# Attention and MLP-mixer on one core: the opening of batches 0 to 2 put in another order (masks sooner, V2 of both heads in one slot, q and k regrouped ahead of the last channel-mix items, part of the kT copies on VectorE)

## The chip, the cores and the metric

The kernel runs on one core of one Trainium2 chip. The time of a run is the device time of that core in microseconds. Each kernel was run several times, always beside runs of the kernel before on the same chip. A run counts as slow when it is over 1.5% longer than the fastest of the same kernel. A difference of less than 2% gets the verdict "same"; a 95% interval goes with every ratio, so that smaller differences can be told apart too.

## The reference, cut to what matters

Eight batches, eight heads, 576 positions, head width 64. Attention with a sliding window of 128 and an ALiBi bias, then an MLP-mixer on its output:

```python
scores = scale * q @ k.T + bias            # rel in [0, 128) only, else -1e9
attn   = exp(scores - max) / sum
x      = attn @ v                          # put back to (batch, 576, 512)
u      = x + (relu(x.T @ w_tok1) @ w_tok2).T      # token mix
out    = u + relu(u @ w_ch1) @ w_ch2              # channel mix
```

## The kernel before: the parts that the change touches

A *group* is one pair of heads of one batch: groups 0 to 3 are batch 0, 4 to 7 batch 1, 8 to 11 batch 2. The kernel runs the attention of one batch beside the mixer of the batch before it. TensorE instructions of the two are interleaved by `spread`, which puts the items of a side list between those of a main list by their costs. In the traces each engine's instructions come in the order in which they are written.

Names in code and traces: `pe` are the exponentials of the scores and `pb` the same times the mask (a mask product), `xb` is the normalized attention output, `ub` is `u` (its sum with the token mix) and `UT` its transpose, which the channel mix reads. V2 stands for the V matmuls of group 2 with their normalization. A relu eviction takes a finished block of the channel mix out of PSUM.

For batches 0 to 2, q and k come in over the software DMA queue, are regrouped by VectorE (L152), transposed by TensorE (L214) and copied out of PSUM (L226, L227). From batch 3 on, the transposes are done by DMA, which also needs the regrouped data.

```python
def regroup(b, h0, h1, which=(0, 1)):              # VectorE, L152
    for n in which:
        raw, t = ((qn, qg), (kn, kg))[n]
        nc.vector.tensor_copy(out=t[:RP, :, h0:h1, :], in_=raw[b % 2]...)   # cut

def att_T(g, early=False):
    ...                                            # 6 + 6 transposes per group
    nc.scalar.copy(out=dst[0], in_=src[0])                              # qT, ScalarE
    (nc.scalar.copy if early or b == 2 else nc.vector.tensor_copy)(out=dst[1], in_=src[1])  # kT

def att_V(g, early=False):
    ...                                            # V matmuls, reciprocal, product
    if hp == NHP - 1 and b + 2 < B:                # last group of a batch:
        for c in range(NF):
            dma_v(b + 2, c)                        # its v loads, 2 batches ahead
        dma_v_tail(b + 2)
```

After the opening (batch 0's attention, written out by hand), the channel mix of batch 0 (`c1`) runs beside the attention of batch 1, then the mixer of batch 1 (`its1`) beside that of batch 2:

```python
n0 = 9
for _, f in c1[:n0]:
    f()                                            # channel matmuls alone
side = [(0.0, lambda: regroup(1, 0, H))]
if B > 3:
    side.append((0.0, lambda: dma_qk(3, 0, H)))    # loads of q and k of batch 3
side += [(0.6, lambda: att_T(g)), (0.6, lambda: att_T(g + 1))]
...                                                # scores, transposes, V of batch 1
spread(c1[n0:] + its1[: n1 - 3], side)
for _, f in its1[n1 - 3 : n1]:
    f()
regroup(2, 0, H)

g = 2 * NHP
side = [(0.6, lambda: att_T(g)), (0.6, lambda: att_T(g + 1))]
side += score_items(g)
side += [(0.6, lambda: att_T(g + 2)), (0.6, lambda: att_T(g + 3))]
for n in range(2):
    side.append((0.3, lambda n=n: regroup(3, 0, H, (n,))))
    side.append((0.0, lambda n=n: dma_trans(3, (n,))))
side.append((0.0, lambda: dma_qk_behind(4, 3)))    # q, k of batch 4 once tk(3) is in
...
spread(its1[n1:], side)
```

The softmax here doesn't subtract the row's maximum and nothing guards it: scores larger than these inputs give would overflow.

## Time and profile before

| | |
|---|---|
| median of 3 runs | 313.87 us (313.83 to 314.05) |
| TensorE busy | 93% of a span of 311.7 us |
| VectorE, ScalarE busy | 56%, 59% |
| TensorE idle from 16 to 80 us | 10.1 us |
| granted TensorE clock | 1.00 in every stretch |

The prediction below shows the totals, the table of stretches and the stalls at the transposes. In a table of stretches each line is: the stretch, its length, then busy time (and instructions) of TensorE, weight loads, VectorE, ScalarE and GpSimd, then granted clock, DMA share and GB/s. In a timeline each line is: start, duration, engine, line, operation, output and inputs, count, and in brackets how long the engine was idle just before and what released it.

Three further stalls of TensorE between 40 and 54 us turned out to matter later. They are behind ScalarE's exponentials (`pe`) and VectorE's normalization (`xb`):

```profile
41.84 0.40 PE L246 MATMUL sp<-qT,kT 64*128 64x256 bf16 x4 [0.29 <-ACT pe L258]
...
43.58 0.40 PE L246 MATMUL sp<-qT,kT 64*128 64x256 bf16 x6 [0.76 <-ACT pe L258]
...
53.54 0.73 PE L300 MATMUL ot<-vp,pb 128*128 128x65 bf16 x18 [0.71 <-DVE xb L318]
```

### The profile page before, as it was taken

How to read it: one execution, taken by the hardware profiler on the slowest of the kernel's cores; microseconds unless marked ns; L12 is line 12 of the kernel's file. 1: busy time of each engine (PE TensorE's matmuls, PEld its weight loads, DVE VectorE, ACT ScalarE, POOL GpSimd, SP SyncE). 2: the span in 40 equal slices, each digit the busy share in tenths (PEclk: the TensorE clock that was granted, in tenths of full speed). 3: DMA queues.
4: the chain of work that ended last, by engine and by line, in shares of the span. 5: the costliest groups of instructions: out<-in, count | busy, mean ns of one | idle time of the engine just before them, and what ended most of it. 6: DMA issues, size and time to landing. Idle time of an engine off the chain costs nothing.

```text
span 311.7 us, 6394 instructions
## 1 busy us (share of the span) xinstructions
PE 290.3 (93%) x2645; PEld 182.8 (59%) x2669; DVE 176.0 (56%) x341; ACT 185.1 (59%) x371; POOL 61.8 (20%) x85
## 2 busy tenths in 40 slices
PE   6877888898999999999999999999999999999995
PEld 2465655455764467645774467645774477547743
DVE  6695667658466865378733865378434753262021
ACT  3974496185997438854896438853996338304700
POOL 8993242600202500540013000500000000000000
PEclk9999999999999999999999999999999999999999
DMA  7999999998596997699649027781101110101022
GB/s 95 151 181 205 201 169 171 194 102 180 94 159 128 190 144 124 99 218 198 138 78 109 34 91 107 90 80 68 37 0 36 67 69 0 36 34 70 0 69 101
DMA packets 83005, 33.64 MB, mean 108 GB/s; under 512 B 62048, under 2 KB 78496, under 8 KB 82976
## 3 DMA queue, kind: packets, MB, share of 16 engines
q0 software_dynamic: 54224, 17.90, 56.2%
q1 hardware_dynamic: 28752, 15.34, 20.0%
q8 instruction: 21, 0.34, 0.5%
q14 instruction: 8, 0.07, 0.1%
HBM read 35.78 MB, written 9.44 MB: 145 GB/s over the span
## 4 chain that ended last, share of the span: by engine, by line
PE 66%; ACT 20%; DVE 9%; issue 4%
PE o L471 26%; PE ct L439 20%; ACT pe L258 10%; ACT R L450 5%; PE ot L300 4%; PE ht L376 4%; PE sp L246 3%; PE t L363 3%; ACT qT L226 2%; DVE pb L269 2%; PE ut L426 2%; ACT r1t L368 2%; DVE xb L311 1%; PE wt L597 1%; DVE qg L152 1%
## 5 line engine op out<-in xcount | busy, mean ns | idle before, releaser
L258 ACT ACTIVATE pe<-sp,biascol 128x512 bf16<-128x512 f32 x128 | 80.7, 705 | 47.0 <-PE sp L246 47.0
L439 PE MATMUL ct<-UT,WC 128*128 128x288 bf16 x768 | 103.0, 286 | 2.8 <-ACT R L450 2.1
L471 PE MATMUL o<-WC,R 128*128 128x512 bf16 x402 | 99.2, 379 | 1.0
L439 PEld LDWEIGHTS <-WC 128*128 128x128 bf16 x768 | 72.5, 98 | 25.0 <-issue 5.7
L450 ACT ACTIVATE R<-ct 128x288 bf16<-128x288 f32 x180 | 67.2, 434 | 32.4 <-PE ct L439 28.1
L269 DVE TENSOR_TENSOR pb<-pe,masks 128x1024 bf16<-128x1024 bf16 x64 | 44.0, 688 | 47.9 <-ACT pe L258 47.9
L471 PEld LDWEIGHTS <-R 128*128 128x128 bf16 x420 | 39.0, 98 | 42.0 <-issue 0.9
L137 POOL DMA_DIRECT2D vp<-in_v_dram x28 | 25.7, 935 | 74.0 <-PE ot L300 63.2
L380 DVE TENSOR_TENSOR ub<-ht,xb 128x512 bf16<-128x512 f32 x35 | 24.0, 688 | 14.9 <-PE ht L376 14.8
L483 DVE TENSOR_TENSOR obt<-o,ub 128x512 f32<-128x512 f32 x31 | 21.3, 687 | 17.2 <-PE o L471 17.2
L300 PEld LDWEIGHTS <-pb 128*128 128x128 bf16 x576 | 21.8, 98 | 6.5 <-DVE xb L318 0.8
L300 PE MATMUL ot<-vp,pb 128*128 128x65 bf16 x576 | 23.4, 194 | 1.2 <-DVE xb L318 0.7
L246 PE MATMUL sp<-qT,kT 64*128 64x256 bf16 (+2 forms) x320 | 21.5, 250 | 3.1 <-ACT pe L258 1.5
L226 ACT COPY qT<-tq 128x576 bf16<-128x576 bf16 x20 | 24.2, 1208 | 0.0
L318 DVE TENSOR_TENSOR xb<-ot,rt 128x640 bf16<-128x640 f32 x28 | 23.1, 825 | 1.0
L246 PEld LDWEIGHTS <-kT 64*128 64x128 bf16 x320 | 12.5, 94 | 17.0 <-issue 12.0
L376 PE MATMUL ht<-r1t,W 128*128 128x512 bf16 x66 | 20.5, 379 | 0.8 <-ACT r1t L368 0.7
L368 ACT ACTIVATE r1t<-t 128x512 bf16<-128x512 f32 x14 | 8.4, 600 | 16.0 <-PE t L363 15.9
L363 PE MATMUL t<-xb,W 128*128 128x512 bf16 x69 | 16.2, 379 | 0.1
L317 DVE RECIPROCAL rt<-ot 128x10 f32<-128x10 f32 x28 | 6.1, 217 | 15.6 <-PE ot L300 15.6
L431 DVE COPY UT<-ut 128x576 bf16<-128x576 bf16 x28 | 11.5, 450 | 4.8 <-PE ut L426 4.8
L479 DVE COPY obt<-o 128x512 f32<-128x512 f32 x4 | 2.8, 692 | 19.7 <-PE o L471 19.7
(68 smaller groups left out, 200.7 us busy)
## 6 DMA issues: line engine op xcount, KB each, us to landing
out_dram<-obt SPq DMA_DIRECT2D x31, 256.0 KB, 2.1
qn<-in_q_dram POOLq DMA_DIRECT2D x7, 576.0 KB, 11.8
kn<-in_k_dram POOLq DMA_DIRECT2D x7, 576.0 KB, 14.3
vp<-in_v_dram POOLq DMA_DIRECT2D x28, 128.0 KB, 11.3
WC<-in_moe_w_ch_dram POOLq DMA_DIRECT2D x3, 512.0 KB, 7.7
WC<-in_moe_w_ch_dram POOLq DMA_DIRECT2D x1, 1536.0 KB, 22.5
out_dram<-obt SPq DMA_DIRECT2D x10, 128.0 KB, 2.4
vp<-in_v_dram POOLq DMA_DIRECT2D x16, 64.0 KB, 5.4
```

Source lines behind the costliest of these rows:

```text
L137: nc.gpsimd.dma_start(out=vp[b % 2][:, :, c, 0:D], in_=v[b, :, c * P : (c + 1) * P, :].rearrange("h s d -> s h d"),)
L226: nc.scalar.copy(out=dst[0], in_=src[0])
L246: nc.tensor.matmul(sp[:, hh, i * 256 + x0 : i * 256 + x1], lhsT=kt[r, k0 : k0 + P], rhs=qt[r, q0 : q0 + x1 - x0], start=True, stop=True,)
L258: nc.scalar.activation(out=pe[:, i, :], in_=sp[:, i, :], func=ACT.Exp, bias=biascol[:, h : h + 1], scale=scale,)
L269: nc.vector.tensor_tensor(out=pb[:, :, :].rearrange("p h (k x) -> p h k x", k=2), in0=pes.pop((g, half))[:, :, :].rearrange("p h (k x) -> ...
L300: nc.tensor.matmul(ots[i][:, qb * (D + 1) : (qb + 1) * (D + 1)], lhsT=pb[:, i, col : col + P], rhs=vb[:, h, kc, :], start=(n == 0), stop=( ...
L363: nc.tensor.matmul(t1[:, :], lhsT=W1[:, c, dh * P : (dh + 1) * P], rhs=xb[b][:, c, :], start=(c == 0), stop=(c == NCH - 1),)
L376: nc.tensor.matmul(ht[:, :], lhsT=W2[:, j, c0(c) : c0(c) + P], rhs=r1s[b, j][:, :], start=(j == 0), stop=(j == NDH - 1),)
L380: nc.vector.tensor_tensor(out=ubs[b][:, c, :], in0=ht[:, :], in1=xb[b][:, c, :], op=ALU.add)
L439: nc.tensor.matmul(ct[:, :], lhsT=WC1[:, cb, ht_i * P : (ht_i + 1) * P], rhs=UT[:, cb, o : o + SH], start=(cb == 0), stop=(cb == NCB - 1),)
L450: nc.scalar.activation(out=r2, in_=ct[:, :], func=ACT.Relu)
L471: nc.tensor.matmul(o2[0][:, :], lhsT=R2[:, ht_i, col : col + P], rhs=WC2[:, ht_i, :], start=(ht_i == 0 and c != NF), stop=(ht_i == NHT - 1),)
```

## The change

Its intent is to take work off the path that TensorE waits for in the first 75 us: masks of the last two groups sooner on VectorE, kT copies from ScalarE to VectorE where ScalarE is the busier, regroupings before the work that they can hide behind. The core of the diff (the opening cut to the order of its calls):

```diff
-        (nc.scalar.copy if early or b == 2 else nc.vector.tensor_copy)(out=dst[1], in_=src[1])
+        on_act = g in (0, 3, 10, 11)
+        (nc.scalar.copy if on_act else nc.vector.tensor_copy)(out=dst[1], in_=src[1])
 ... the copy of UT out of PSUM: batch 0's last one goes to VectorE
-        (nc.vector.tensor_copy if b else nc.scalar.copy)(
+        (nc.scalar.copy if b == 0 and cb < NCB - 1 else nc.vector.tensor_copy)(
 ... opening
+        build_masks(2)
         att_M(0, 1)
         att_T(2, True)
-        build_masks(2)
 ...
+        build_masks(3)
         att_M(1, 1)
         att_T(3, True)
         att_V(0, True)
-        build_masks(3)
 ...
-        att_V(2, True)
         trans_u(0, 0)
+        att_M(3, 1)
+        att_V(2)
         tok2_pair(1)
-        att_M(3, 1)
 ... (tok1_pair(3), tok2_pair(3), trans_u(0, 2), trans_u(0, 3) reordered alike)
 ... batch 1
-        n0 = 9
+        n0 = 11
 ...
-        spread(c1[n0:] + its1[: n1 - 3], side)
-        for _, f in its1[n1 - 3 : n1]:
+        spread(c1[n0:] + its1[: n1 - 2], side)
+        regroup(2, 0, H)
+        for _, f in its1[n1 - 2 : n1]:
             f()
-        regroup(2, 0, H)
 ... batch 2
-        side = [(0.6, lambda: att_T(g)), (0.6, lambda: att_T(g + 1))]
-        side += score_items(g)
-        side += [(0.6, lambda: att_T(g + 2)), (0.6, lambda: att_T(g + 3))]
+        side = [(0.3, lambda n=n: att_T(g + n, n % 2 == 1)) for n in range(NHP)]
         for n in range(2):
-            side.append((0.3, lambda n=n: regroup(3, 0, H, (n,))))
+            side.append((0.2, lambda n=n: regroup(3, 0, H, (n,))))
             side.append((0.0, lambda n=n: dma_trans(3, (n,))))
         side.append((0.0, lambda: dma_qk_behind(4, 3)))
+        side += score_items(g)
```

More of the change, by code (lines that the diff above doesn't have):

```diff
@@ L647 @@
         att_M(3, 0)
-        att_V(2, True)
         trans_u(0, 0)
+        att_M(3, 1)
+        att_V(2)
         tok2_pair(1)
-        att_M(3, 1)
+        att_V(3, True)
         tok1_pair(2)
-        att_V(3, True)
         trans_u(0, 1)
+        tok1_pair(3)
         tok2_pair(2)
-        tok1_pair(3)
+        tok2_pair(3)
         trans_u(0, 2)
-        tok2_pair(3)
+        trans_u(0, 3)
         nc.vector.tensor_copy(out=swap[:, 0:TAIL], in_=ident[:, TAIL:P])
         nc.vector.tensor_copy(out=swap[:, TAIL:P], in_=ident[:, 0:TAIL])
-        trans_u(0, 3)
         c1, its1 = mixer_items(0)[-2 * NHT :], mixer_items(1, lead=2)
         n1, g = 6, NHP
-        n0 = 9
+        n0 = 11
         for _, f in c1[:n0]:
```

## The prediction

> **What bounds the kernel now.** I read the engine totals first, then the busy tenths by slice, then stretches of the span, then the order of single instructions where TensorE is idle, and last the DMA issues with their times to landing.
>
> From the page, the totals (busy us, share) and the slices (7.8 us each, tenths busy):
>
> ```profile
> PE 290.3 (93%) x2645; PEld 182.8 (59%) x2669; DVE 176.0 (56%) x341; ACT 185.1 (59%) x371; POOL 61.8 (20%) x85
> ...
> PE   6877888898999999999999999999999999999995
> ...
> DMA  7999999998596997699649027781101110101022
> ```
>
> TensorE is the bound after slice 9, and the DMA engines are nearly full up to slice 9. All the edits act before about 76 us, so they can only remove TensorE idle time there. The stretches (PE is the second number after the length) say how much there is:
>
> ```profile
> 16.00:24.00 8.00, 5.66 (x105) 4.92 (x105) 7.83 (x22) 5.93 (x12) 8.00 (x12) 1.00 1.49 184
> 24.00:32.00 8.00, 6.15 (x79) 4.88 (x80) 3.93 (x11) 3.17 (x7) 2.67 (x4) 1.00 1.29 204
> 32.00:40.00 8.00, 6.87 (x74) 4.83 (x72) 5.33 (x9) 4.19 (x9) 1.37 (x2) 1.00 1.24 203
> 40.00:48.00 8.00, 6.84 (x77) 4.74 (x76) 5.74 (x11) 7.60 (x16) 4.21 (x5) 1.00 2.20 167
> 48.00:56.00 8.00, 7.18 (x104) 4.48 (x105) 6.64 (x14) 3.77 (x8) 1.55 (x2) 1.00 2.30 159
> 56.00:64.00 8.00, 6.57 (x49) 3.19 (x49) 3.80 (x6) 2.95 (x6) 5.27 (x5) 1.00 1.64 210
> 64.00:72.00 8.00, 7.08 (x65) 3.97 (x66) 6.40 (x10) 5.20 (x9) 0.00 (x0) 1.00 1.01 89
> 72.00:80.00 8.00, 7.57 (x85) 4.97 (x84) 5.34 (x11) 5.47 (x12) 0.00 (x0) 1.00 0.88 181
> ```
>
> Eight minus the PE numbers: 2.34, 1.85, 1.13, 1.16, 0.82, 1.43, 0.92, 0.43; sum 10.1 us. That is the ceiling. Two per cent of 313.87 is 6.3 us, so a clear win needs well over half of it. From 16 to 24 VectorE is busy 7.83 of 8: it is what TensorE waits for. From 40 to 48 ScalarE is (7.60 of 8).
>
> The single stalls, from TensorE's timeline (bracket: idle before, and releaser):
>
> ```profile
> 30.03 4.69 PE L439 MATMUL ct<-UT,WC 128*128 128x288 bf16 x37 [0.36 <-ACT UT L431]
> 35.16 0.43 PE L214 MATMUL tT<-ident,qg 96*128 96x96 bf16 x6 [0.44 <-DVE qg L152]
> 36.28 0.43 PE L214 MATMUL tT<-ident,kg 96*128 96x96 bf16 x6 [0.70 <-DVE kg L152]
> ...
> 59.94 0.43 PE L214 MATMUL tT<-ident,qg 96*128 96x96 bf16 x6 [0.57 <-DVE qg L152]
> 61.18 0.43 PE L214 MATMUL tT<-ident,kg 96*128 96x96 bf16 x6 [0.81 <-DVE kg L152]
> ...
> 71.53 0.23 PE L422 MATMUL ut<-swap,ub 128*128 128x128 bf16 x1 [0.79 <-DVE ub L380]
> ```
>
> The regroupings of batch 1 (35 us) and batch 2 (60 us) each stall the transposes that read them. Last, the two loads of batch 3 that the change wants sooner, from the DMA issues between 48 and 52 us (last number: median us to landing):
>
> ```profile
> qn<-in_q_dram POOLq DMA_DIRECT2D x1, 576.0 KB, 13.1
> ...
> kn<-in_k_dram POOLq DMA_DIRECT2D x1, 576.0 KB, 15.5
> ```
>
> Issued at 48.43 and 50.44, they land at about 61.5 and 65.9. I return to this under step 4.
>
> **What the Trainium skill says.** "Perfetto Trace Analysis", Optimizing Scalar/DVE Operations: an access to PSUM costs VectorE some 125 ns and ScalarE some 51 ns. The trace agrees in sign: the copy of a transposed 128x576 tile out of PSUM takes 0.76 us on VectorE (kT) and 0.64 us on ScalarE (qT). So moving kT copies is no saving of work, only of ScalarE's place in line. "DMA: Bandwidth & Descriptors", Queues, rings and completion order: each DMA engine serves its queues in turn, packet by packet. So a hardware transpose beside the software queue slows both; before, the first transposes (70.86 us) come when the software queue is nearly empty (10 GB/s in 68 to 70), so the trace neither confirms nor denies it. "TensorE: Matmul & The Clock Gate", What's actually happening: about 3.4 us of idleness halves the clock. No stall in this trace is that long, and the clock reads 1.00 in every stretch.
>
> **The change part by part.** I followed the order of the changed kernel's instructions on each engine and put the durations of this trace on them by hand.
>
> *Step 1, first scores (0 to 17 us).* Two kT copies (groups 1 and 2) leave ScalarE: each took about 0.53 us start to start there. Exponentials wait for them, so the third group's first exponential starts some 0.6 us sooner (13.8 instead of 14.4). But VectorE gains two copies (0.67 start to start), and the masks of heads 6 and 7 (six instructions, about 0.68 us start to start when undisturbed, 11.83 to 12.51 for the pair before) now stand ahead of the first normalization. Summing VectorE's queue from 9.3 us: copy 9.95, mask product 10.56, regrouping 11.17, masks 11.85, product 12.45, copy 13.12, product 13.72, regrouping 14.28, masks 14.96, product 15.57, then four normalizing instructions (1.26): 16.85 against 16.57 before. Nothing gained for the first token-mix matmul, some 0.3 us lost.
>
> *Step 2, token mix of batch 0 (17 to 30 us).* Masks are out of the way, the two products of group 3 sit together, V2 in the shared slot needs one reciprocal and one product (0.98 us start to start) instead of two of each (1.26), and the third token-mix matmul no longer stands ahead of V3. Following the chain: second half of group 3's scores 19.3 (19.45 before), its products done 21.85, V2 normalized 22.9, ub of pair 1 23.65, V3 normalized 24.9 (25.9 before), pair 3's ub 27.7 (28.7 before), transposes of the last column block 28.3, UT copy on VectorE about 0.45 instead of 0.64. The channel mix then runs freely at 28.8 instead of 30.03: **1.2 us gained.**
>
> *Step 3, batch 1.* Before, 40 channel matmuls come ahead of the first transposes; now 48, and VectorE's order puts six relu evictions (four before) ahead of the regrouping. At 0.1225 us each 45 matmuls from 28.8 end near 34.4, so the regrouping starts at 34.85 (34.15 before), q is ready at 35.8 and k at 36.95. The stall is about 1.4 + 0.8 = 2.2 us against 1.14: **the 1.1 us comes back off.** Eight more matmuls are done, though, so first exponential is only 0.6 later (39.65 against 39.06). The stretch from there is ScalarE's: 16 exponentials at 0.575, two q copies at 0.55 and now four instead of six evictions at 0.3, so it ends near 51.2 instead of 51.77. Then the regrouping of batch 2 stands ahead of the last eight channel matmuls and the first tok1: VectorE's normalizations end at 56.4, q and k are ready at 57.4 and 58.5, and TensorE arrives at 57.95. Stalls of 0.57 + 0.81 shrink to some 0.1. By the first-group transposes of batch 2 TensorE is at 58.9 where it had been at 61.6: **2.5 us gained in all,** of which 1.2 from step 2 and about 1.3 from the moved regrouping.
>
> *Step 4, batch 2.* All four transposes now come before the scores, with two of the four kT copies on VectorE, and the regrouping of batch 3 directly behind. VectorE works in order, and its order is now: q of batch 3, first ub, **k of batch 3**, four ub with two products and one eviction between. k cannot start before its load lands at 65.9, whatever TensorE does, as the DMA queue ahead of it is full from the start. From there: regrouping 1.0 (66.9), two ub 1.2 (68.1), product, eviction, product 1.8 (69.9), two ub 1.2, so **the u transposes start near 71.3, against 71.53 before.** TensorE reaches them at about 68.2 and waits some 3 us. So most of the 2.5 us is spent on waiting for a load that nobody waited for before (k was regrouped at 71.39). What remains is work done ahead: group 9's scores before u, group 8's V and group 10's scores before the channel mix. From 71.3 the blocks add up to a channel mix at 75.35; twelve matmuls (1.47) bring it to 76.85, and the same content was reached at 78.42 before. **Net 1.6 us.**
>
> Behind 80 us nothing is removed. ScalarE was 9.94 of 10 busy from 80 to 90; with two groups of exponentials already done, part of TensorE's 0.3 + 0.38 us idle up to 100 may go: 0.2.
>
> **The rivals.**
> (a) The 2.5 us carries through, because k lands sooner or the ub work hides it: 311.3 or a little less. For it: a stall that I place by hand could be short. Against it: landing is set by a queue full from 4 us on.
> (b) The wait becomes worse. The transpose of q of batch 3 now starts near 63.2, beside the last 2.7 us of the load of k. If they share engines packet by packet, k lands 1 to 2 us later, everything after it too, and the gain is gone: 313.5 to 314.5. A stall of 5 us could moreover halve the clock for a window: about 1.7 us more, an estimate from the skill's 3.4 us. Against it: the load may be nearly over, and the transpose's first packets come late.
> (c) The kT copies make VectorE the bound in the first 25 us and step 2 gives nothing. VectorE is already 7.83 of 8 busy there. It matters little to the end if step 4's wait stands, which absorbs the loss as it absorbs the gain.
>
> **Range and chances.** Steps 1 to 4 give 1.6 + 0.2 = 1.8, so 312.1 if the load of k is undisturbed. I take off about 0.5 for (b), half likely at around 1 us: **312.6 us.** Rival (a) with an extra microsecond gives the lower end, 310.7; (b) in full the upper one, 314.4. Faster by over 2% means under 307.6, half of all idle time there gone: 0.04. Slower by over 2% means 320.1, which needs both parts of (b) several times over: 0.02.
>
> **What would show it.** Right: the free-running channel mix of batch 0 starts near 28.8; the stalls at the batch 1 transposes grow to about 2 us; those at batch 2's vanish; kg's third large copy starts at 66 to 67 with VectorE idle before it, released by the DMA; the u transposes of batch 1 start near 71.3 after about 3 us of idle TensorE. Wrong: u transposes at 69 (then (a)) or at 73 and later (then (b)); a start of the channel mix at 29.5 or later (then (c)).

## The result, and the profile after

| | median | range | runs | ratio to before, 95% |
|---|---|---|---|---|
| before | 313.94 us | 313.83 to 314.05 | 4 | |
| changed | 311.97 us | 310.94 to 312.50 | 4 | 0.9933 (0.9906 to 0.9960) |

All runs were fast ones, though one of the changed kernel had a clock of 0.994 (312.50). A ratio is the mean time of one kernel's fast runs over that of the other's in the same rounds, so it isn't quite the ratio of the medians. The change is worth 0.7%, some 2 us. That is a real gain, close to the predicted 312.6.

What follows first is the profiled run of the changed kernel (312.24 us), the one that the prediction's working can be laid beside. In the changed kernel's profile, line numbers from L227 on are one higher than before. TensorE is busy 290.9 us (94% of a span of 310.4). The stretches of the changed kernel, columns as before:

```profile
16.00:24.00 8.00, 6.58 (x124) 5.62 (x124) 7.41 (x17) 5.24 (x11) 8.00 (x13) 1.00 1.31 150
24.00:32.00 8.00, 6.46 (x72) 5.09 (x70) 3.94 (x10) 3.36 (x8) 2.72 (x4) 1.00 1.28 204
32.00:40.00 8.00, 5.89 (x63) 4.25 (x62) 5.35 (x9) 2.91 (x8) 1.92 (x2) 1.00 1.23 195
...
56.00:64.00 8.00, 7.66 (x80) 4.60 (x78) 6.23 (x9) 4.15 (x8) 4.92 (x5) 1.00 1.62 197
64.00:72.00 8.00, 5.76 (x41) 2.49 (x41) 6.14 (x11) 5.19 (x9) 0.00 (x0) 1.00 1.87 133
72.00:80.00 8.00, 7.95 (x102) 6.04 (x102) 5.86 (x13) 4.26 (x11) 1.73 (x3) 1.00 0.91 188
```

TensorE's busy time rose from 5.66 to 6.58 in 16 to 24, from 6.57 to 7.66 in 56 to 64 and from 7.57 to 7.95 in 72 to 80. It fell from 6.87 to 5.89 in 32 to 40, and from 7.08 to 5.76 in 64 to 72. So the time won in two places was partly spent in two others. TensorE's timeline says on what:

```profile
28.87 5.67 PE L440 MATMUL ct<-UT,WC 128*128 128x288 bf16 x45 [0.18 <-DVE UT L432]
...
35.96 0.43 PE L214 MATMUL tT<-ident,qg 96*128 96x96 bf16 x6 [1.41 <-DVE qg L152]
37.08 0.43 PE L214 MATMUL tT<-ident,kg 96*128 96x96 bf16 x6 [0.70 <-DVE kg L152]
...
59.57 0.43 PE L214 MATMUL tT<-ident,kg 96*128 96x96 bf16 x6 [0.29 <-DVE kg L152]
...
68.28 1.02 PE L472 MATMUL o<-WC,R 128*128 128x512 bf16 x4 [0.70 <-DVE ub L381]
...
71.88 0.23 PE L423 MATMUL ut<-swap,ub 128*128 128x128 bf16 x1 [1.49 <-DVE ub L381]
```

The free-running channel mix starts at 28.87 instead of 30.03. The stalls of the first transposes of batch 1 grow from 0.44 + 0.70 to 1.41 + 0.70. Those of batch 2 shrink from 0.57 + 0.81 to 0.29. Then come two waits for `ub`, 0.70 and 1.49, where there was one of 0.79. VectorE's timeline tells why `ub` is late. It sat idle before the regrouping of k of batch 3, and what ended that was a DMA:

```profile
63.26 0.95 DVE L152 COPY qg<-qn 96x3072 bf16<-96x3072 bf16 x1 [1.13 <-PE tT L214]
...
66.67 0.95 DVE L152 COPY kg<-kn 96x3072 bf16<-96x3072 bf16 x1 [1.86 <-DMA kn<-in_k_dram]
```

And the chain of waits, followed back from the end (start, length, what), now runs through two loads, q of batch 2 (issued at 32.26) and k of batch 3 (issued at 51.48, when q had landed), into the `ub` additions and the `u` transposes:

```profile
32.26 18.66 DMA qn<-in_q_dram
...
51.48 15.10 DMA kn<-in_k_dram
...
66.67 0.95 DVE kg L152
```

Over the whole span that chain is put down as 61% TensorE and 17% DMA. Before it was 66% TensorE, 20% ScalarE and 9% VectorE, with no DMA at all.

To compare many kernels I cut the span at three landmarks. A is the start of the free-running channel mix of batch 0, u the first `u` transposes of batch 1, D the first matmul of batch 1's shared last output chunk. From D to the end all kernels took 218.7 to 218.8 us (one took 219.6, told below), so everything happens ahead of D.

| profiled run | A | A to u | u to D | A to D | idle at batch 1's first transposes | clock of the run |
|---|---|---|---|---|---|---|
| before | 30.03 | 41.50 | 21.47 | 62.97 | 1.14 | 1.000 |
| changed | 28.87 | 43.01 | 19.74 | 62.75 | 2.11 | 1.000 |
| changed, again | 29.73 | 42.83 | 19.74 | 62.57 | 1.85 | 0.994 |

From A to D the changed kernel is only 0.2 us shorter in this run, so nearly all of the profiled run's 1.3 us had been won before A. Of the rest, 1.7 us come from u to D and 1.5 are lost again from A to u.

### The profile page after: what moved, and what is told of

Same layout as the page of the kernel before. It is cut to its first block, busy times and chain, and to the rows that moved or that the text cites. A ratio compares the mean times of both kernels' runs of the same rounds, so it can differ in the third digit from the quotient of the medians.

```text
span 310.4 us, 6391 instructions
## 1 busy us (share of the span) xinstructions
PE 290.9 (94%) x2645; PEld 183.3 (59%) x2669; DVE 179.1 (58%) x344; ACT 182.0 (59%) x366; POOL 61.5 (20%) x85
## 4 chain that ended last, share of the span: by engine, by line
PE 61%; DMA 17%; ACT 13%; POOL 4%; issue 2%; DVE 2%; POOLq 0%; DVEq 0%
PE o L472 25%; PE ct L440 18%; DMA qn<-in_q_dram 10%; DMA kn<-in_k_dram 7%; ACT pe L259 5%; ACT R L451 5%; PE ht L377 4%; PE ot L301 4%; PE t L364 3%; PE sp L247 3%; PE ut L427 2%; ACT qT L226 2%; ACT r1t L369 2%; POOL vp L143 1%; PE o2h L497 1%
## 5 line engine op out<-in xcount | busy, mean ns | idle before, releaser
L381 DVE TENSOR_TENSOR ub<-ht,xb 128x512 bf16<-128x512 f32 x35 | 23.9, 687 | 10.6 <-PE ht L377 10.5
L319 DVE TENSOR_TENSOR xb<-ot,rt 128x640 bf16<-128x640 f32 x29 | 23.9, 824 | 1.0
```

What stands on the lines that cost most here:

```text
L319: nc.vector.tensor_tensor(out=xs, in0=o4[:, :, :, 0:D], in1=rt[:, :, :, None].broadcast_to([P, 2, NCH, D]), op=ALU.mult,)
```

## The experiments

Twelve kernels ran, one of them the changed kernel again, in three calls (kernel before in each: medians 313.78, 313.69 and 313.45 us). The first two calls were on one chip and the third on another. The theory going in was that of the prediction. The moved regroupings win some 2 to 2.5 us in batches 1 and 2, VectorE's wait for the load of k takes most of it back, and therefore the opening's gain is swallowed too. The rivals were that the batch 1 stall is to blame, that the batch 2 list as such is no gain, and that the load is slower than before.

| kernel | median | range | fast/all runs | ratio, 95% |
|---|---|---|---|---|
| late_k | 313.30 | 312.32 to 314.58 | 6/6 | 0.9980 (0.9948 to 1.0013) |
| qk3_first | 311.23 | 310.58 to 312.06 | 6/6 | 0.9906 (0.9875 to 0.9937) |
| without_step4 | 313.40 | 312.59 to 314.22 | 6/6 | 0.9979 (0.9948 to 1.0010) |
| old_prologue | 313.14 | 311.93 to 315.03 | 6/6 | 0.9970 (0.9934 to 1.0006) |
| changed_again | 312.45 | 311.51 to 312.98 | 6/6 | 0.9952 (0.9936 to 0.9968) |
| filled_stall | 311.97 | 311.01 to 315.68 | 5/6 | 0.9948 (0.9917 to 0.9979) |
| old_prologue_filled | 313.10 | 311.67 to 318.03 | 4/6 | 0.9957 (0.9934 to 0.9980) |
| best1 | 308.68 | 308.15 to 309.19 | 4/4 | 0.9838 (0.9823 to 0.9853) |
| prologue_only | 312.81 | 312.51 to 313.05 | 5/5 | 0.9975 (0.9963 to 0.9987) |
| regroup2_only | 311.59 | 311.32 to 311.85 | 5/5 | 0.9938 (0.9926 to 0.9950) |
| n0_9 | 312.19 | 311.51 to 314.46 | 6/6 | 0.9972 (0.9946 to 0.9998) |
| best2 | 307.89 | 307.73 to 307.98 | 4/4 | 0.9820 (0.9807 to 0.9833) |

Medians and ranges are over all runs, ratios over the fast ones. All results were correct.

### First call: what is the wait for the load worth?

**late_k.** The regrouping of batch 3 in the changed kernel goes behind the scores of two groups, so that VectorE no longer stands in front of a load that has not landed:

```diff
         side = [(0.3, lambda n=n: att_T(g + n, n % 2 == 1)) for n in range(NHP)]
+        side += score_items(g) + score_items(g + 1)
         for n in range(2):
             side.append((0.2, lambda n=n: regroup(3, 0, H, (n,))))
 ...
         side.append((0.0, lambda: dma_qk_behind(4, 3)))
-        side += score_items(g)
```

> The changed kernel with only the regrouping of batch 3 (q and k) moved back behind the scores of two groups, so that VectorE does not meet it before the ub work. Theory (the wait for the load of k of batch 3 gives back what was gained earlier): the idle time of VectorE on that load is gone, the u transposes of batch 1 start near 69.8 us instead of 71.88, and the kernel takes about 310.0 us (ratio to the kernel before 0.987 to 0.989). Rival (the ub work or TensorE itself holds the u transposes, the load only looks like the cause): u transposes still at 71.5 or later, and 311.7 to 312.2 us (ratio 0.993 to 0.995).

Measured: 313.30, ratio 0.9980 with an interval that holds 1, and a miss of over 3 us against the theory. (Two of the six runs had a clock of 0.995; the four others took 312.32 to 313.46, a miss as well.) The wait for the load was gone from VectorE, but `u` was no sooner: it came at 71.98, with TensorE idle 1.79 us on `ub`. Group 9's mask products had moved in among the `ub` additions (four mask products between the first and the last of them instead of two), and one of them held VectorE idle for 1.00 us until its exponential was there. The regrouping then also came so late that the next loads, which are issued only after it (the gate opened at 82.22, against 76.20 in the changed kernel), landed late in turn. VectorE waited 0.91 us for that q (regrouped at 88.81) and 0.84 us for that k (at 93.28). These two waits are new, and D to the end took 219.6 us here instead of 218.7. So "take the wait away" isn't the same as "regroup later": the early regrouping also pays for the loads behind it. The experiment had moved two things.

**qk3_first.** The loads themselves come sooner. q and k of batch 3 are issued ahead of v of batch 2 and not behind it, with the order of all engines' work left as in the changed kernel:

```diff
-        if hp == NHP - 1 and b + 2 < B:
+        if hp == NHP - 1 and 0 < b and b + 2 < B:      # v of batch 2 not here
 ...
             side.append((0.0, lambda: dma_qk(3, 0, H)))
+            def v2():
+                for c in range(NF):
+                    dma_v(2, c)
+                dma_v_tail(2)
+            side.append((0.0, v2))
```

> The changed kernel with its instruction order on TensorE, VectorE and ScalarE kept, and only the DMA issue order changed: the loads of q and k of batch 3 ahead of the loads of V of batch 2. Theory (it is the landing of k that VectorE waits for): k lands some 4 us sooner (near 62), its regrouping starts right behind the first ub near 64.8, u transposes near 70.0, about 310.1 us (ratio 0.987 to 0.990). Rival (order on VectorE as such costs the time, not the load): no change against the changed kernel, 311.8 (ratio 0.993). Second rival (V of batch 2 now comes late): group 8's V waits near 72 us and the time is 312 or more.

Measured: 311.23, ratio 0.9906. VectorE now goes from `ub` straight into k:

```profile
65.61 0.68 DVE L381 TENSOR_TENSOR ub<-ht,xb 128x512 bf16<-128x512 f32 x1
66.21 0.95 DVE L152 COPY kg<-kn 96x3072 bf16<-96x3072 bf16 x1
```

No bracket stands behind the second line: the load had landed. A to u fell from 43.01 to 41.18 and A to D from 62.75 to 60.92. This is the cleanest evidence for the wait: with only the order of loads changed, 1.8 us come back (0.25 of it is a smaller stall at batch 1's transposes, 1.86 for 2.11). That compares one profile with one profile. The times show less: these six runs took 311.26 us in the mean, the five runs of the changed kernel with a clock of 0.998 or more (in two other calls) 311.65, so 0.4 us less. Not every run of the changed kernel need have had the wait (see changed_again). The run itself missed its expected 310.1.

**without_step4.** The changed kernel with the old list for batch 2 and all its kT copies on ScalarE:

```diff
-        on_act = g in (0, 3, 10, 11)
+        on_act = g in (0, 3) or b == 2
 ...
-        side = [(0.3, lambda n=n: att_T(g + n, n % 2 == 1)) for n in range(NHP)]
+        side = [(0.6, lambda: att_T(g)), (0.6, lambda: att_T(g + 1))]
 ... (the rest of the list as in the kernel before)
```

> The changed kernel with the batch 2 part undone (transposes, kT copies and regrouping of batch 3 in the places of the kernel before), prologue and moved regrouping of batch 2 kept. Theory (the gain is made by 60 us, some 1.6 us by the profile, and the batch 2 part neither makes nor saves it): 312.2 us, ratio 0.993 to 0.996. Rival (early transposes of batch 2 are what pays): 313.3 us, ratio 0.997 or more.

Measured: 313.40. The new batch 2 list is thus worth having, wait and all: about 1 us, comparing runs at full clock (312.59, 312.76 and 312.86 here; 311.51 and 311.88 of the changed kernel in the second call). But the runs fell in two clusters. Three of them, near 314.0, had a mean clock of 0.992 to 0.993. The three others were at 0.998 to 1.0. That was new, and no theory had it.

**old_prologue.** The opening of the kernel before, everything else changed:

```diff
 # against the kernel before: only these parts of the change
+        on_act = (early and b == 0) or g in (10, 11)
+        n0 = 11
+        ... regroup(2, 0, H) ahead of the last two items; the new batch 2 list
```

> The changed kernel with the old prologue of batch 0 (masks, V2, token mix, kT copies of batch 0 all on ScalarE), everything from the channel mix on as changed. Theory (TensorE has some 2 us of idle time at the ub wait, so 1.2 us lost in the prologue is absorbed there): 311.5 to 312.3 us, ratio 0.992 to 0.995, as the changed kernel. Rival (the parts add up): the 1.2 us are lost, 313.1 us, ratio 0.997 or more.

Measured: 313.14, but again two of six runs at a clock of 0.995 (313.18 and 313.43), and one at 315.03 without such a cause. The scatter is larger than the question asked of it, so nothing follows from the median.

### Second call: the clock

**changed_again.** The changed kernel, unedited.

> The changed kernel itself, once more, as the measure for the three that run beside it. The granted clock of single runs is what matters: theory (the stall at the first transposes of batch 1, 1.41 + 0.70 us, nearly without TensorE work for 2.1 us, lets the clock drop to half for a while in some executions): runs at a mean clock of 0.997 to 1.000 take 310.9 to 312.0 us, runs at 0.992 to 0.996 take 1 to 1.5 us more. Rival (the spread comes from the landing of loads alone): no relation between clock and time within the kernel.

Measured: 312.45. Four of the six runs had a mean clock of 0.994 or 0.995, at 312.35 to 312.98. The two others, at 0.999 and 1.0, took 311.51 and 311.88. The profile was one of the four (stretches, columns as before; the clock is the number after the last bracket):

```profile
36.00:38.00 2.00, 0.74 (x13) 0.60 (x14) 1.63 (x2) 0.00 (x0) 0.00 (x0) 1.00 1.24 208
38.00:40.00 2.00, 2.00 (x20) 1.63 (x18) 0.76 (x1) 1.05 (x2) 0.00 (x0) 0.50 1.27 203
40.00:42.00 2.00, 2.00 (x13) 1.03 (x11) 0.97 (x2) 1.05 (x2) 0.00 (x0) 0.65 2.87 151
```

and in its timeline, the lines just ahead of that:

```profile
36.82 0.43 PE L214 MATMUL tT<-ident,qg 96*128 96x96 bf16 x6 [1.41 <-DVE qg L152]
37.69 0.43 PE L214 MATMUL tT<-ident,kg 96*128 96x96 bf16 x6 [0.44 <-DVE kg L152]
37.95 1.13 PE L440 MATMUL ct<-UT,WC 128*128 128x288 bf16 x4
```

The clock is halved for about 3.4 us (0.50 over one stretch of 2 us; 0.65 in the next, which is 1.4 us of half clock). It begins right after the two stalls at the first transposes of batch 1, 1.41 and 0.44 us, and the four channel matmuls of the third line take 1.13 us, where the same four took 0.66 in the run at full clock. There was no wait for k of batch 3 in this run, and A to D is 62.57, nearly that of the run that had the wait and not the half clock (62.75). The lateness of TensorE is not needed to explain that: k was issued at 49.88 and had landed at 64.3 here, against 51.48 and 66.6 there, and VectorE wanted it at 64.8 there. So in its two profiles the changed kernel lost its gain in two different ways, and its median hides which.

The profiles of without_step4 and old_prologue, both with a clock under 1, show the same: stalls of 1.42 and 0.44, and of 1.41 and 0.44 us at the first transposes of batch 1, then half clock from about 37.9 to 41.3 and from about 38.6 to 42.0. But late_k (1.60 and 0.43) and qk3_first (1.42 and 0.44) had such stalls and a clock of 1.000.

**filled_stall.** To take the idle time away without changing the work, six useless 128x512 matmuls stand ahead of those transposes:

```diff
+        side.append((0.0, lambda: warm(6)))
         side += [(0.6, lambda: att_T(g)), (0.6, lambda: att_T(g + 1))]
```

> The changed kernel with six matmuls of no use (128x512, some 0.22 us each) ahead of the first transposes of batch 1, in the place of TensorE's 1.41 us of idle time. Theory (that idle time at times costs the clock): no run below a clock of 0.997, spread narrower, median 311.2 to 311.6 us, 0.3 to 0.8 us under the changed kernel beside it. Rival (no relation): same as the changed kernel or slower by up to the 1.3 us that they take.

Measured: 311.97 (one of six runs slow, 315.68 at 0.987). Four of the five fast runs took 311.01 to 312.21, at a clock of 0.999 or 1.0. The fifth, the profiled one, took 314.44 at full clock. Its load of k held VectorE longer than in any other profile. VectorE:

```profile
68.96 0.96 DVE L152 COPY kg<-kn 96x3072 bf16<-96x3072 bf16 x1 [3.02 <-DMA kn<-in_k_dram]
```

TensorE was then idle 1.94 and 1.49 us on `ub`, u stood at 74.17, and A to D was 64.01. Expected were 311.2 to 311.6 and no run under a clock of 0.997, so both were missed. One run of six at a low clock, against four of six in changed_again, points to the idle time, but the next kernel shows that the filling alone doesn't settle it.

**old_prologue_filled.** The same six matmuls in old_prologue.

> The changed kernel with the old prologue of batch 0, and with the same six matmuls, so that the clock does not confuse the comparison. Theory (the prologue's 1.2 us are absorbed by the later wait for k of batch 3): within 0.4 us of the filled_stall kernel. Rival (parts add up): 1.0 to 1.3 us slower than it, so 312.3 to 312.9 us.

Measured: fast runs 311.67, 311.77, 312.47 and 313.72, and two slow ones (316.56 at a clock of 0.994, 318.03 at 0.988). Filled or not, two of six runs with the old opening had a low clock. By their ratios, the fast runs are 0.1% from those of filled_stall, but the intervals overlap over most of their width. Whether the opening's gain is swallowed by a wait further on, as the prediction held, can't be read from this pair. Its profile, with neither a half clock nor a wait for the load, gives A to D as 60.93, the same as qk3_first. That is the distance when neither loss occurs.

**best1.** The changed kernel with qk3_first's order of loads, the loads of q and k of batch 1 put ahead of the last third of WC1, and the regrouping of batch 1 put between the evictions of the channel mix instead of behind them:

```diff
             if n == 2:
+                dma_qk(1, 0, H)                 # before: behind the third WC1 load
 ...
-        n0 = 11
-        for _, f in c1[:n0]:
+        n0 = 9
+        for i, (_, f) in enumerate(c1[:n0]):
             f()
-        side = [(0.0, lambda: regroup(1, 0, H))]
+            if i in (3, 7):
+                regroup(1, 0, H, (i // 4,))
+        side = []
```

> An attempt to beat both: the changed kernel with the loads of q and k of batch 3 ahead of V of batch 2, the loads of q and k of batch 1 ahead of the last third of the first channel weights, and the two regroupings of batch 1 placed in the middle of the channel evictions (behind the fourth and the eighth), transposes two evictions sooner. Theory (the stalls of the changed kernel at 36 and 68 us are waits for loads and for VectorE's order): stall at the first transposes of batch 1 under 0.6 us instead of 2.1, none on the load of k of batch 3, 309.3 to 310.3 us. Rival (ScalarE's exponentials are the bound from 40 to 52 us, so an earlier start only moves the idle time): 310.8 to 311.3.

Measured: 308.68, ratio 0.9838, better than expected, and clocks of 0.998 to 1.0 in all runs. The stall at batch 1's transposes is 0.18 us instead of 2.1, the wait at u 0.79, and A to D 57.93.

### Third call: the parts alone

**prologue_only.** The kernel before with nothing but the new opening.

```diff
 # against the kernel before
+        on_act = g in (0, 3) or b == 2
+        ... the new order of the opening, up to the last trans_u(0, 3); n0 = 9 and all behind as before
```

> The kernel before with the new prologue of batch 0 alone (masks sooner, V2 in the shared slot, kT copies of groups 1 and 2 and the last UT copy on VectorE); nine evictions ahead and both regroupings in their old places. Theory from the profiles so far (the chain from the second k load to the first token-mix matmul is some 0.6 us longer, the chain from there to the free channel mix 1.4 shorter, and the load of k of batch 1, which lands near 34 to 35 us, holds the next step): free channel mix 0.4 to 0.8 us sooner than 30.03, and most of it given back at the regrouping of batch 1: 313.2 to 313.6 us, ratio 0.998 to 1.000. Rival (it carries through as predicted for step 2): 312.6, ratio 0.996.

Measured: 312.81, ratio 0.9975: 0.8 us, in five runs within 0.6 us of each other. A was 29.30 and A to D 62.78 (62.97 before). The gain was carried to the end, which is the rival's reading and not mine.

**regroup2_only.** The kernel before with a single edit, the regrouping of batch 2 moved ahead of the last two items (eight channel matmuls and the first tok1 block are still behind it):

```diff
-        spread(c1[n0:] + its1[: n1 - 3], side)
-        for _, f in its1[n1 - 3 : n1]:
+        spread(c1[n0:] + its1[: n1 - 2], side)
+        regroup(2, 0, H)
+        for _, f in its1[n1 - 2 : n1]:
             f()
-        regroup(2, 0, H)
```

> The kernel before with the regrouping of batch 2 alone moved ahead of the last two channel items of the first output chunks. Theory (it takes the 0.57 + 0.81 us of stalls out of the path, and k of batch 3 is regrouped late enough not to wait): 312.3 to 312.7 us, ratio 0.995 to 0.997. Rival (VectorE's ub chain behind it sets the u transposes anyway): 313.4 us or more, ratio 0.999.

Measured: 311.59, ratio 0.9938. This edit is worth 1.9 us, as much as the whole change, and more than expected. All stalls of TensorE from 30 to 72 us that are left:

```profile
35.54 0.43 PE L214 MATMUL tT<-ident,qg 96*128 96x96 bf16 x6 [0.44 <-DVE qg L152]
36.71 0.43 PE L214 MATMUL tT<-ident,kg 96*128 96x96 bf16 x6 [0.74 <-DVE kg L152]
...
44.04 0.40 PE L246 MATMUL sp<-qT,kT 64*128 64x256 bf16 x6 [0.48 <-DVE kT L227]
...
69.42 0.23 PE L422 MATMUL ut<-swap,ub 128*128 128x128 bf16 x1 [0.79 <-DVE ub L380]
```

The edit does two things, though. By `n1 - 2` the list that `spread` mixes with the attention of batch 1 is also one item longer, which moves the attention to other places between the channel matmuls. It begins behind the first transposes, where four channel matmuls followed in the kernel before and eight do now. Before:

```profile
36.55 0.66 PE L439 MATMUL ct<-UT,WC 128*128 128x288 bf16 x4
```

regroup2_only:

```profile
36.98 1.15 PE L439 MATMUL ct<-UT,WC 128*128 128x288 bf16 x8
```

The 0.57 + 0.81 at batch 2's transposes are gone, as meant. So is the 0.71 on `xb`, and 0.29 + 0.76 on the exponentials became 0.48 on kT. A to D is 60.48, against 62.97 before and 62.75 in the changed kernel. Of these 2.5 us, 0.9 are won before batch 2's transposes (57.62 minus A of 30.41 for the first tok1 matmul, 58.13 minus 30.03 before), where the regrouping of batch 2 can have no part yet. So the moved line and the longer list share the gain, and no run has one without the other. VectorE takes k of batch 3 at 69.27 here, behind a `ub`, with the load long landed.

**n0_9.** The changed kernel with nine instead of eleven channel-mix items ahead of batch 1's regrouping.

```diff
-        n0 = 11
+        n0 = 9
```

> The changed kernel with nine channel evictions, as before, instead of eleven ahead of batch 1. Theory (the eleven make the stall of 1.41 + 0.44 us or more during which the clock at times drops to half, 38 to 42 us): no run at a clock of 0.996 or less, 311.2 to 311.8 us, ratio 0.992 to 0.994. Rival (the clock drops whatever this number is): runs at 0.994 remain and the median is 312.2 or more.

Measured: 312.19, ratio 0.9972, no better than the changed kernel, and a miss of the theory in time and clock. Five runs of six kept their clock; one had 0.988 and took 314.46. The stall didn't shrink (0.59 and 1.66 us), but its cause is another. VectorE:

```profile
33.70 1.10 DVE L152 COPY qg<-qn 96x3072 bf16<-96x3072 bf16 x1
35.94 0.96 DVE L152 COPY kg<-kn 96x3072 bf16<-96x3072 bf16 x1 [1.14 <-DMA kn<-in_k_dram]
```

k of batch 1 had not landed. The new opening brings the kernel to this point sooner than the load does, which the order of loads in best1 avoids. In prologue_only, with the same opening and the same nine items, the profile shows no such wait (0.44 + 0.50 us of TensorE idle there), so it comes and goes between runs.

**best2.** best1 with the masks of the last two heads back at their old place, behind the V matmuls of group 0, as the traces showed the first token-mix matmul later in every kernel with the new place:

```diff
-        build_masks(3)
         att_M(1, 1)
         att_T(3, True)
         att_V(0, True)
+        build_masks(3)
```

> The best kernel so far with the masks of heads 6 and 7 put back behind the first normalization, as they were before the change, so that the first token-mix matmul does not wait for them. Theory (these masks stand in VectorE's line ahead of it and cost about 0.6 us, which nothing later absorbs now): free channel mix 0.4 to 0.7 us sooner, 308.0 to 308.4 us. Rival (the products behind the masks are then late by as much): 308.7 or more.

Measured: 307.89, ratio 0.9820 (0.9807 to 0.9833), with four runs within 0.25 us. This is the best kernel, 5.6 us under the kernel before of its call, and better than the changed kernel. It and best1 ran in different calls, so their difference of 0.2% is not settled: the intervals overlap. What its trace has left of stalls from 29.35 (its A) to u:

```profile
34.48 0.43 PE L214 MATMUL tT<-ident,kg 96*128 96x96 bf16 x6 [0.18 <-DVE kg L152]
...
41.80 0.40 PE L247 MATMUL sp<-qT,kT 64*128 64x256 bf16 x6 [0.48 <-DVE kT L228]
...
67.54 0.23 PE L423 MATMUL ut<-swap,ub 128*128 128x128 bf16 x1 [0.78 <-DVE ub L381]
```

## Why the prediction was right, and which terms were off

The time was right (311.97 in the run of the prediction, 312.45 in a second set, against 312.6), and the mechanism named for it was seen. Not all terms were right, and errors offset each other: less was gained before batch 2 than predicted (1.8 us for 2.5), and less was lost by the wait at `u` (2.2 us of idle TensorE for about 3). And the wait stood in three of the six profiles that have the changed kernel's loads and batch 2 list (1.23 to 3.02 us, with k landing at 66.0 to 68.9; the three others had k in at 63.8 to 64.6). The changed kernel has one profile of each kind. That 312.6 came so close is in part luck.

**Step 1, first scores.** Predicted: the first token-mix matmul 0.3 us later, 16.85 against 16.57. Measured: 17.07 against 16.72 in the profile. That was the earliest of the nine profiles with the new opening: their mean is 17.8, with one at 18.8, against 17.0 over four with the old one (16.7 to 17.4). So some 0.8 us are lost, and this term was too small. In the changed kernel's profile VectorE has no idle time from its first kT copy (9.14) on, where it had waits of 0.96 and 0.88 us before, so a late landing of the second load of k goes straight on to the token mix.

**Step 2, token mix.** Predicted A at 28.8, a gain of 1.2 us. In the profile it was 28.87, almost too good: over the nine profiles A is 29.6 in the mean, over the four 30.2. So the gain is nearer 0.6 in the traces, and 0.8 by the times of prologue_only. The chain itself was right: from the first token-mix matmul to A it is 11.8 us in all nine, against 13.0 to 13.3, a gain of 1.2 to 1.5 (predicted 28.8 - 16.85 against 30.03 - 16.57, so 1.5). It is step 1 that takes the rest back. Rival (c) asked for a start at 29.5 or later, a bound in absolute time that the first loads alone can shift by 1 us. It should have been set as a distance from the first scores.

**Step 3, batch 1.** Predicted stalls of 1.4 + 0.8: measured 1.41 + 0.70, then 1.41 + 0.44. The first exponential was predicted at 39.65 and came at 39.86. That TensorE would have the first group's transposes of batch 2 behind it at 58.9 (61.6 before) was not: it was so at 59.84, against 61.66 before. That is 1.8 us gained, and not the 2.5 that the prediction gives (whose own two times differ by 2.7). The first of these transposes starts at 58.86, which looks like the predicted number but is another event. Besides, what failed are two things. First, the sentence that the moved regrouping is worth "about 1.3": the edit is worth 1.9 us alone (regroup2_only), as it also changes how batch 1's attention is interleaved, and VectorE's normalizations and ScalarE's exponentials fell into better places. How much of it is the moved line is not shown. Second, "No stall in this trace is that long", with the clock brought up only for a stall of 5 us at u. In 5 of the 10 runs of the changed kernel, the mean clock was 0.994 or 0.995, and in the one profiled it was the two stalls of step 3 after which the clock was halved, as in the profiles of without_step4 and old_prologue. It costs about 1.0 us (in changed_again, 312.68 mean of four against 311.70 of two; in without_step4, 314.04 against 312.74). No run of regroup2_only, prologue_only, best1 or best2, with 0.2 to 1.2 us of stall there, had a clock under 0.998. But qk3_first, with 1.86 us, didn't either in six runs, and one run of the kernel before, whose profile has 1.14 us of stall, did (316.60 us at 0.993, first call). So the half clock was seen right behind this stall in three profiles of three, but the stall doesn't decide it, and that it is the cause is not shown. The filled kernels don't settle it, and three of the four kernels named (all but best1) ran on the other chip.

**Step 4, batch 2.** Predicted: k regrouped at 66 to 67 with VectorE idle before it, released by the DMA. Measured: 66.67, 1.86 us idle, released by the DMA. Predicted u at 71.3 after about 3 us of idle TensorE: measured 71.88 after 0.70 + 1.49. Net 1.6 us, and 0.2 more behind 80 us: by D it was 1.38 in the profile, of which 0.4 are two waits for ScalarE behind 80 us that are gone (0.24 and 0.16 before). qk3_first showed the cause by taking the wait away with nothing else reordered on the engines. But "most of the 2.5 us is spent on waiting for a load" was seen in the one profile at full clock only. In the other the half clock took the time, and the wait did not occur.

**The absorbed opening.** The working implied, and rival (c) said, that the wait absorbs what the opening gains. In prologue_only, where nobody waits for that load, it is carried through. In the changed kernel, old_prologue_filled against filled_stall leaves it open.

**Rivals.** (a), with its 311.3 us, is about what the kernel does where the load of k comes sooner: 311.23 in qk3_first, with 60.9 from A to D. (b), a load slowed by the transpose of q beside it, was not seen. The load took 15.1 us from issue to landing, 15.5 before, and 13.9 to 16.7 over all profiles with that order of loads. The transpose was the one that was slowed, 9.3 us to landing against 5.0 before, and it is not on the chain. (c) holds in part: VectorE's added work costs the 0.8 us of step 1, but step 2 gains more than that. The 0.5 us taken off for (b) was thus taken off for the wrong reason. The half clock, which costs 1 us in about half of the runs, happens to be the same amount.

**What stays open.** How regroup2_only's 1.9 us divide between the moved line and the interleaving. Why the half clock comes in some runs and not in others of the same kernel, and whether the slow runs of the two filled kernels are of its kind. And whether the rest of best2's gain over regroup2_only (2.6 us in A to D, of which 1.0 is the stall at batch 1's transposes) can be put down to single edits: they weren't run apart.

## What to carry to other kernels

When work is moved ahead on an in-order engine, look at what its inputs wait for: a copy pulled forward past its load's landing holds up all that stands behind it, and the cure is to issue the load sooner, not the copy later (qk3_first gained, late_k lost). Try the parts of a many-part change alone: here a single edit was worth as much as all of them, and the best kernels also had the loads reordered. Look at what else such an edit moves: this one changed the interleaving as well. And when the runs of a changed kernel spread wider than those of the kernel before, read the granted clock of each run ahead of the medians: part of the scatter may be a clock state that the medians mix in.

## What the Trainium skill lacked or had wrong

- "TensorE: Matmul & The Clock Gate", What's actually happening: it gives "≥1 idle window (~3.4µs)" as what halves the clock. Here no stall was that long: the clock was 0.50 after stalls of 1.41 and 0.44 us with six transposes between them, and likewise in two more profiles, and the mean clock was 0.995 or less in 5 of 10 runs of that kernel. Further down, under "A second HAM failure mode: psum-queue depth-cycling", the page does allow for short idle times between groups of matmuls, but gives no length. The page's statement that the window is free-running fits that it comes in some runs only, but no run here shows it. Its other figure agrees: the half clock lasted about 3.4 us (0.50 over 2 us, 0.65 over the next 2).
- "DMA: Bandwidth & Descriptors", Queues, rings and completion order: queues being served in turn doesn't tell who loses. A hardware transpose started beside the end of a large software-queue load took 9.3 us to landing instead of 5.0, while the load took 15.1 instead of 15.5. In filled_stall and n0_9, with the same overlap, the transpose took 10.6 and 8.6; in changed_again and old_prologue, where the load had landed, 5.1 and 5.5.
- No page has it: how much the landing of the same load differs between runs of one program. k of batch 3 landed at 66.6 us in one profile of the changed kernel and at 64.3 in the other (15.1 and 14.4 from its issue), and VectorE waited 1.86 us for it in the first and not at all in the second. In filled_stall it was 68.9 and 3.02.
